# Other products to keep TensorE warm, shorter row-transfer times in the planner, and a new table of ranks

## The chip, the cores and the metric

The kernel runs on one core of a Trainium2 chip. The metric is the device time of one execution in microseconds (us). The kernel before was timed three times; the median is 1224.96 us (1224.6 to 1226.9). Engines are named as in the profile: PE is TensorE (PEld its weight loads), DVE is VectorE, ACT is ScalarE, POOL is GpSimd, SP is SyncE, which issues most DMAs.

## What is computed

A thresholded attention over 8 batches of 8 heads (576 tokens, head size 64), and then a feed-forward layer pair with a quick GELU over the 4608 tokens.

```python
scores = scale * np.matmul(q, k.transpose(0, 1, 3, 2))
thresh = np.max(scores, axis=-1, keepdims=True) - tau
scores = np.where(scores >= thresh, scores, -1000000000.0)
scores = scores - np.max(scores, axis=-1, keepdims=True)
attn = np.exp(scores)
attn = attn / (np.sum(attn, axis=-1, keepdims=True) + 1e-09)
x = np.matmul(attn, v)      # heads side by side: 4608 x 512
...
h = x @ w_in                # 512 x 2048
g = h * (1.0 / (1.0 + np.exp(-1.702 * h)))
return (g @ w_out).astype(np.float32)
```

All products run in FP32. The two weight matrices come as 64-bit floats.

## The kernel before

**Attention.** Two heads make a pair: there are 32 pairs, n = 0 to 31, four to a batch. A pair passes through these steps, each a function of that name:

- SP loads q, k and v (`load_qk`, `load_v`). The first four pairs are turned by TensorE (`turn_in`, L565 and L568) and copied out of PSUM by ScalarE (`turned`, L580) or VectorE (L578); later ones are transposed by VectorE (`prep`, L556).
- `scores_run` (L590) makes nine groups of scores, in the four 64 x 64 quadrants of the array at once. ScalarE copies each group to SBUF (`keep`, L607), VectorE takes maxima of blocks (`in_groups`, L613) and joins them (`over_tiles`, L622; `cross_max` on ScalarE, L632; `over_halves`, L639).
- The threshold has to be spread over the partitions. For pairs 1 and 3 to 6 that goes through DRAM: `turn_rows` (L646, L647) makes a row, `row_out` (L663) writes it, `row_in` (L672) reads it back to many partitions, and `add_row` (L678) adds it to two of the five score tiles by DMA. For pairs 0 to 7 these DMAs are issued by POOL. Pairs 0, 2 and 7 onwards use a VectorE transpose (`spread_max`, L651).
- `sub` (L687, VectorE) applies the threshold, `mask` (L694) and `exps` (L698) run on ScalarE, five tiles each. For pairs 0 to 3 TensorE makes the sums (`sums_by_pe`) and for all pairs the values (`values`), both through L709. `place_x` (L813) multiplies by the reciprocal and writes the input of the feed-forward part.

**Feed-forward.** 18 blocks of 256 tokens. The first two go together: `mm1_ahead` (L876) and `mm1_0` (L887), then the second layer (L856). They need pairs 0 to 3 placed and the first pieces of w_in. Later blocks use Strassen-like sums with seven products instead of eight (L955, L1097, L1248, L1357, L1397). From the seventh pair on, values of one pair and scores of the next run together on TensorE.

**Weights.** 16 pieces of w_in, then 16 of w_out, in 512 columns each, are loaded in that order (`load_w`, L510) and turned into FP32 by two ScalarE operations (`cv_power` L520, `cv_power2` L524) and two VectorE operations (`cv_whole` L538, `cv_end` L545).

**Warm products.** `run_up` (L1457) runs 32 product records on ones at the start. `stay_warm` (L1463) is a task of two products of 64 x 64 ones by 64 columns, both in the same quadrant of the array; each FP32 product leaves two records in the trace. 44 such tasks (`WARM`) stand behind pair 1's turned q and k, with the last rank of all. Their output is never read.

**The order.** The order on every engine is fixed when the kernel is built, by a planner in the kernel's own text, `run_in_order`. Every piece of work is a `task` with an engine, a cost in us, a rank, the tasks it comes after, and buffers that it takes and gives back (counted in `limits`). The planner plays time forward: whenever an engine is free it takes, among its tasks that are ready and whose buffers are free, the one with the lowest rank, and issues it. On the chip the engines then run these orders, each instruction waiting for what it really depends on.

The rank of an attention task is the pair's number plus a bias by function: `EARLY` for pairs 0 to 3, `SECOND` for 4 to 7, `LATER` above. `CV` biases the weight tasks, whose base goes linearly through `W_RANK` (first four pieces of w_in, the other twelve, w_out). `L_RANK` adds to the loads of q, k and v of pairs 0 to 7. Tasks of the feed-forward part have either the first rank of all (`FIRST`, -9) or 1000 (TensorE). Warm tasks have 1001.

DMA transfers are planned as tasks of two movers, DMS (queue of SP) and DMW (queue of POOL). For a row they are `row_out`'s issue, a transfer of 0.3 us with a lag, `row_in`'s issue, and a transfer of 1.1 us with a lag; `rq` holds for each pair the engine, a factor on the issue cost, the mover and the second lag, and `flow` an extra for the busy early stretch.

Of the kernel before, what the change touches and what calls it, by code (L numbers as in the profile page):

```python
# [21 lines left out]
P = 128  # L22
# [10 lines left out]
def kernel(  # L33
# [77 lines left out]
    ones = const.tile([P, D], FP32, name="ones")  # L111
# [7 lines left out]
    eye = const.tile([P, P], FP32, name="eye")  # L119
# [10 lines left out]
    for x in ("raw0", "raw1", "qkT0", "qkT1", "mb"):  # L130
# [3 lines left out]


    EARLY = {
        "add_row": 53.65,
        "cross_max": 41.92,
        "exps": 6.51,
        "in_groups": -32.22,  # L140
        "keep": -15.97,
        "load_qk": -22.11,
        "load_v": 171.75,
        "mask": 55.94,
        "one_row": -16.46,
        "over_halves": 4.98,
        "over_tiles": 6.84,
        "place_x": 20.81,
        "row_in": 57.26,
        "row_out": 46.57,  # L150
        "scores_run": -10.81,
        "spread_max": 80.7,
        "spread_sums": 100.15,
        "sub": 57.71,
        "sums_by_pe": -23.63,
        "turn_in": 17.28,
        "turn_rows": 22.22,
        "turned": 23.53,
        "values": 13.65,
    }  # L160
    SECOND = {
        "add_row": 56.43,
        "cross_max": 3.09,
        "cross_sums": 16.09,
        "exps": 52.27,
        "in_groups": 30.05,
        "keep": -234.91,
        "load_qk": -13.08,
        "load_v": -27.45,
        "mask": 33.62,  # L170
        "over_halves": 278.98,
        "over_tiles": -10.26,
        "place_x": -25.62,
        "prep": 26.79,
        "row_in": -17.52,
        "row_out": -29.19,
        "scores_run": -37.55,
        "spread_max": 47.26,
        "sub": 30.71,
        "sums_in": 55.32,  # L180
        "sums_out": 55.2,
        "turn_rows": -18.94,
        "turn_sums": 6.04,
        "values": -8.21,
    }
    LATER = {
        "add2": -48.46,
        "add3": -25.71,
        "copy2": 39.6,
        "copy3": -20.1,  # L190
        "cross_max": -23.15,
        "cross_sums": -92.97,
        "exps": 55.84,
        "in_groups": 20.69,
        "keep": -228.95,
        "load_qk": -18.31,
        "load_v": 17.97,
        "mask": 2.33,
        "over_halves": -43.91,
        "over_tiles": 0.85,  # L200
        "place_x": -1.66,
        "prep": 50.01,
        "s_level1": -3.36,
        "s_level2": -12.87,
        "scores_run": 9.86,
        "silu2": 26.22,
        "spread_max": 3.4,
        "sub": 4.36,
        "sums_in": 25.12,
        "sums_out": 39.44,  # L210
        "turn_sums": 63.21,
        "values": -6.31,
    }
# [34 lines left out]
    def transfer(by, time, a, kind=0, give=(), lag=1.7):  # L248
        return task(by, time, FIRST, moved, kind, after=[a], give=give, lag=lag)
# [1209 lines left out]
    def stay_warm(x):  # L1459

        d = psM.tile([P, BANK], FP32, name="up", tag="mo")
        for _ in range(2):
            nc.tensor.matmul(d[0:D, 0:D], lhsT=ones[0:KT], rhs=ones[0:KT], start=True, stop=True)  # L1463

    def tau_terms():

# [23 lines left out]
    ROWS_BY_POOL = range(8)  # L1490
# [38 lines left out]
    warmth = [task("PE", 4.4, -20.0, run_up, take=("psM",), give=("psM",))]  # L1529
# [760 lines left out]
    for n in range(NP):  # L2290
        gate = per_pair * (n - LEAD)
        assert gate < len(ffn) or gate <= 0
        after = [ffn[gate]] if gate >= 0 and ffn else []
        r = float(n)

        slow = 1.1 if n < 2 * NPAIR else 1.0
        rq = ("POOL", 1.4, "DMW", 2.2) if n in ROWS_BY_POOL else ("SP", 1.0, "DMS", 1.7)
        flow = 2.9 if n in (0, 1, 4) else 0.0
        by_sp = n not in ROWS_BY_POOL
        q0, q1 = (nc.scalar, nc.scalar) if n == 0 else (nc.sync, nc.sync)  # L2300

# [48 lines left out]
        if n >= JOINT:  # L2350

            a = None
            for t in range(NKT + 1):
# [12 lines left out]
                a = w  # L2366
                for j in js:
# [6 lines left out]
                    a = w  # L2374
# [141 lines left out]
```

## Time and profile before

| what | value |
|---|---|
| median of 3 runs | 1224.96 us (1224.6 to 1226.9) |
| the profiled execution | 1225.39 us |
| its span, first to last instruction | 1223.6 us |
| mean granted TensorE clock | 0.999 |
| records of L1463 (warm products) | 176, from 21.5 to 74.3 us, 13.1 us busy |
| records of L1457 (first products) | 32, 3.7 us busy |

How to read the profile: busy time of an engine is the time in which at least one of its instructions runs; a row of a stretch gives its borders and length, then busy time and number of instructions of PE, PEld, DVE, ACT and POOL, the granted TensorE clock, the busy share of the DMA engines and GB/s. A row of the timeline gives start, length, engine, line, operation, output and input, the number of instructions merged in it, and in brackets how long the engine stood idle before and what ended that. A row by line ends with busy time, mean ns of one, and idle time before it. Matmuls overlap, so their mean duration is longer than their share of the engine's time; rates are taken from rows with many records.

### The profile page before, as it was taken

How to read it: one execution, taken by the hardware profiler on the slowest of the kernel's cores; microseconds unless marked ns; L12 is line 12 of the kernel's file. 1: busy time of each engine (PE TensorE's matmuls, PEld its weight loads, DVE VectorE, ACT ScalarE, POOL GpSimd, SP SyncE). 2: the span in 40 equal slices, each digit the busy share in tenths (PEclk: the TensorE clock that was granted, in tenths of full speed). 3: DMA queues.
4: the chain of work that ended last, by engine and by line, in shares of the span. 5: the costliest groups of instructions: out<-in, count | busy, mean ns of one | idle time of the engine just before them, and what ended most of it. 6: DMA issues, size and time to landing. Idle time of an engine off the chain costs nothing.

```text
span 1223.6 us, 26039 instructions
## 1 busy us (share of the span) xinstructions
PE 1212.8 (99%) x10592; PEld 987.0 (81%) x10592; DVE 1059.3 (87%) x1649; ACT 803.1 (66%) x1203; POOL 71.0 (6%) x115
## 2 busy tenths in 40 slices
PE   9989999999999999999999999999999999999998
PEld 6857764597978888888777777778787797999998
DVE  6899966678898998898699977998799889999797
ACT  7999976676766756684786468756875676440340
POOL 0112231110000000000000000001100000000000
PEclk9999999999999999999999999999999999999999
DMA  7957779862323232224323252225322341444443
GB/s 203 252 108 199 196 146 190 209 100 58 101 49 110 49 116 56 75 77 126 101 66 103 71 128 76 65 65 128 91 50 67 101 125 50 129 130 141 141 134 103
DMA packets 202232, 137.12 MB, mean 112 GB/s; under 512 B 146880, under 2 KB 164416, under 8 KB 201984
## 3 DMA queue, kind: packets, MB, share of 16 engines
q1 hardware_dynamic: 189712, 110.21, 33.5%
q0 software_dynamic: 11712, 24.95, 10.1%
q8 instruction: 83, 1.36, 0.5%
q10 hardware_dynamic: 688, 0.30, 0.1%
q14 instruction: 37, 0.30, 0.1%
HBM read 103.28 MB, written 23.75 MB: 104 GB/s over the span
## 4 chain that ended last, share of the span: by engine, by line
PE 92%; ACT 4%; DMA 2%; DVE 1%; issue 0%; SPq 0%; POOL 0%; POOLq 0%
PE ops L1397 24%; PE pv L709 10%; PE ps L590 10%; PE hps L955 7%; PE hps L1097 7%; PE ps L955 5%; PE ps L1097 5%; PE ops L856 5%; PE hps L887 4%; PE ops L1357 4%; PE hps L1248 4%; PE ps L1357 3%; PE ps L1248 3%; ACT arena L694 1%; ACT arena L698 1%; ACT arena L607 1%
## 5 line engine op out<-in xcount | busy, mean ns | idle before, releaser
L613 DVE TRANSPOSE_TENSOR_REDUCE part<-arena 128x36 f32<-128x1152 f32 (+1 forms) x300 | 363.8, 1239 | 65.9 <-ACT arena L607 49.0
L607 ACT COPY arena<-ps 128x576 f32<-128x576 f32 x288 | 170.5, 644 | 96.8 <-PE ps L590 96.8
L694 ACT ACTIVATE arena<-arena 128x1152 f32<-128x1152 f32 (+1 forms) x160 | 165.1, 1060 | 67.7 <-DVE arena L687 67.5
L687 DVE TENSOR_TENSOR arena<-arena 128x1152 f32<-128x1152 f32 (+1 forms) x150 | 180.9, 1240 | 3.4 <-DMA arena<-row 2.8
L698 ACT ACTIVATE arena<-arena,shift 128x1152 f32<-128x1152 f32 (+1 forms) x160 | 180.5, 1154 | 1.5
L590 PE MATMUL ps<-arena 64*64 64x288 f32 x2304 | 171.4, 408 | 3.4 <-ACT arena L607 3.1
L1397 PE MATMUL ops<-w_out,arena 128*128 128x256 f32 x768 | 174.4, 381 | 0.0
L1397 PEld LDWEIGHTS ops<-w_out,arena 128*128 128x128 f32 x768 | 144.3, 190 | 24.9 <-issue 5.3
L709 PE MATMUL pv<-arena 64*64 64x288 f32 x2176 | 158.5, 405 | 0.0
L590 PEld LDWEIGHTS ps<-arena 64*64 64x64 f32 x2304 | 82.2, 132 | 64.1 <-ACT arena L607 25.3
L709 PEld LDWEIGHTS pv<-arena 64*64 64x64 f32 x2176 | 82.2, 133 | 52.2 <-issue 9.1
L1397 PE MATMUL ops<-arena 128*128 128x256 f32 x528 | 118.1, 379 | 0.0
L1397 PEld LDWEIGHTS ops<-arena 128*128 128x128 f32 x528 | 100.2, 190 | 14.0 <-issue 0.4
L1262 ACT COPY arena<-hps 128x512 f32<-128x512 f32 x44 | 25.7, 584 | 58.4 <-PE hps L1248 58.3
L632 ACT ACTIVATE other<-red,minus_gap 32x18 f32<-32x18 f32 x118 | 36.2, 307 | 39.0 <-DVE red L622 37.6
L856 PE MATMUL ops<-w_out,arena 128*128 128x512 f32 x128 | 55.9, 595 | 0.0
L1074 POOL DMA_DIRECT2D arena<-wrow x36 | 19.4, 540 | 596.8 <-DMA arena<-in_k_dram 299.6
L887 PE MATMUL hps<-xT,w_in 128*128 128x256 f32 x232 | 50.8, 380 | 0.0
L887 PEld LDWEIGHTS hps<-xT,w_in 128*128 128x128 f32 x232 | 43.9, 190 | 6.8 <-issue 0.4
L856 PEld LDWEIGHTS ops<-w_out,arena 128*128 128x128 f32 x128 | 24.1, 190 | 30.1 <-issue 29.5
L955 PEld LDWEIGHTS hps<-xT,w_in 128*128 128x128 f32 x384 | 44.2, 192 | 1.1 <-issue 0.9
L955 PE MATMUL hps<-xT,w_in 128*128 128x128 f32 x384 | 44.9, 275 | 0.0
(228 smaller groups left out, 1922.2 us busy)
## 6 DMA issues: line engine op xcount, KB each, us to landing
arena<-in_v_dram SPq DMA_DIRECT2D x128, 144.0 KB
arena<-exu SPq DMA_DIRECT2D x42, 256.0 KB
arena<-ext SPq DMA_DIRECT2D x39, 256.0 KB
arena<-wrow POOLq DMA_DIRECT2D x36, 256.0 KB, 3.0
arena<-in_k_dram SPq DMA_DIRECT2D x112, 72.0 KB
arena<-in_q_dram SPq DMA_DIRECT2D x112, 72.0 KB
out_dram<-osb SPq DMA_DIRECT2D x28, 256.0 KB
arena<-row_s SPq DMA_DIRECT2D x48, 144.0 KB
```

The source lines that it names most:

```text
L590: nc.tensor.matmul(ps[ts(c, KT), h, 0:SH], lhsT=mats[n, 1][ts(h, D), ts(j, KT)], rhs=mats[n, 0][ts(h, D), ts(c, SH)], start=True, stop=True,)
L607: nc.scalar.copy(out=sT[n, t][:, u], in_=pss.pop((n, j))[:, :, 0:SH])
L613: nc.vector.tensor_reduce(out=stats[n, op][:, t * 2 * QB : min(2 * t + 2, NK) * QB], in_=sT[n, t].rearrange("p u h (g d) -> p (u h g) d", ...
L687: engine.tensor_tensor(out=s, in0=s, in1=mbs[n].unsqueeze(1).to_broadcast(list(s.shape)), op=ALU.add if n in BY_DMA else ALU.subtract,)
L694: nc.scalar.activation(out=s, in_=s, func=AF.Prelu, alpha=STEEP)
L698: nc.scalar.activation(out=s, in_=s, func=AF.Exp, scale=SCALE, bias=shift)
L709: nc.tensor.matmul(o[c][ts(h, D), 0:SH], lhsT=left(j, h)[ts(c, KT)], rhs=sT[n, t][ts(c, KT), u, h, :], start=(j == 0), stop=(j == NK - 1),)
L856: nc.tensor.matmul(acc[i], lhsT=g0[:, j, ts(i, P)], rhs=w_out[:, j, :], start=(j == 0), stop=(j == NFC - 1),)
L887: nc.tensor.matmul(hidden[j][:, ts(i, BLK)], lhsT=w_in[:, c, ts(j, P)], rhs=xTs[i][:, c, :], start=(c == 0), stop=(c == NDC - 1), skip_gro ...
L955: nc.tensor.matmul(o[:, ts(j, HT)], lhsT=left[:, c, ts(4 * y + j, P)], rhs=right[:, c, :], start=(x in (P1, P2, P5) and j + c == 0), stop= ...
L1097: nc.tensor.matmul(o[:, ts(j, BLK)], lhsT=left[:, c, ts(j, P)], rhs=right[:, c, :], start=(x in (P1, P2, P5) and j + c == 0), stop=(j + c ...
L1397: nc.tensor.matmul(banks[blk][k][:, ts(o, HM)], lhsT=left[:, j, :], rhs=right[:, j, :], start=(j == 0), stop=(j == HF - 1),)
```

## The change

The warm products use two diagonal quadrants in turn, 128 columns of the identity wide; there are 40 tasks instead of 44, planned at 0.24 us instead of 0.26.

```diff
     def stay_warm(x):
         d = psM.tile([P, BANK], FP32, name="up", tag="mo")
-        for _ in range(2):
-            nc.tensor.matmul(d[0:D, 0:D], lhsT=ones[0:KT], rhs=ones[0:KT], start=True, stop=True)
+        for r in range(2):
+            nc.tensor.matmul(
+                d[ts(r, KT), 0:P], lhsT=ones[ts(r, KT)], rhs=eye[ts(r, KT)], start=True, stop=True
+            )
...
-    WARM = 44
+    WARM = 40
...
-                    "PE", 0.26, LAST + 1.0, stay_warm, x, after=warmth[:1] + [pq, pk],
+                    "PE", 0.24, LAST + 1.0, stay_warm, x, after=warmth[:1] + [pq, pk],
```

The planner's figures for the row transfers of pairs whose rows go by POOL become shorter; `flow` no longer holds for pair 4.

```diff
-        rq = ("POOL", 1.4, "DMW", 2.2) if n in ROWS_BY_POOL else ("SP", 1.0, "DMS", 1.7)
-        flow = 2.9 if n in (0, 1, 4) else 0.0
+        rq = ("POOL", 1.4, "DMW", 1.0) if n in ROWS_BY_POOL else ("SP", 1.0, "DMS", 1.7)
+        flow = 2.9 if n in (0, 1) else 0.0
...
-            a = transfer(rq[2], 0.3 + 0.4 * by_sp, task(rq[0], 0.65 * rq[1], r, row_out, n, after=[a]), lag=1.7 - 0.4 * by_sp + flow)
+            a = transfer(rq[2], 0.3 + 0.4 * by_sp, task(rq[0], 0.65 * rq[1], r, row_out, n, after=[a]), lag=1.3 + flow)
```

All tables of ranks are replaced. The entries that the prediction speaks of, and some beside them:

```diff
     EARLY = {
-        "in_groups": -32.22,
-        "mask": 55.94,
-        "scores_run": -10.81,
-        "spread_max": 80.7,
-        "sub": 57.71,
-        "sums_by_pe": -23.63,
-        "turn_in": 17.28,
-        "values": 13.65,
+        "in_groups": 34.28,
+        "mask": 36.88,
+        "scores_run": -51.59,
+        "spread_max": 71.02,
+        "sub": -16.81,
+        "sums_by_pe": 32.0,
+        "turn_in": 64.69,
+        "values": 84.4,
...
     SECOND = {
-        "exps": 52.27,
-        "keep": -234.91,
-        "mask": 33.62,
-        "prep": 26.79,
-        "scores_run": -37.55,
+        "exps": 388.41,
+        "keep": -169.42,
+        "mask": 33.53,
+        "prep": 138.87,
+        "scores_run": 61.18,
...
     LATER = {
-        "over_halves": -43.91,
-        "prep": 50.01,
-        "sums_in": 25.12,
+        "over_halves": -352.38,
+        "prep": 370.61,
+        "sums_in": -380.05,
...
     CV = {
-        "cv_end": 32.35,
-        "cv_power": 11.31,
-        "cv_power2": 54.89,
-        "cv_whole": 26.47,
-        "load_w": 23.87,
+        "cv_end": -85.19,
+        "cv_power": -24.57,
+        "cv_power2": 42.72,
+        "cv_whole": 54.77,
+        "load_w": 75.9,
...
-    W_RANK = (76.72, 196.12, 138.01, 508.95, -9.25, -19.99)
+    W_RANK = (0.79, 73.66, 64.74, 576.72, -32.54, 123.84)
...
-    L_RANK = (3.45, -109.6, -17.9, 36.14, 35.53, 42.62, 27.86, 146.49, 9.14, 81.46, 255.02, -17.35, -3.34, -15.75, -2.02, -2.69, 30.05, -3.25, -48.27, 6.8, -9.58, 10.21, 37.91, -22.41)
+    L_RANK = (-12.89, -5.54, 219.74, 60.65, 2.71, 44.19, 8.15, 170.96, -56.11, 65.12, 219.59, 54.4, 32.1, -27.46, 84.01, -13.31, 4.97, 33.77, 16.65, 59.15, -8.32, 117.45, -4.08, 3.78)
```

More of the change, by code (lines that the diff above doesn't have):

```diff
@@ L136 @@
     EARLY = {
-        "add_row": 53.65,
-        "cross_max": 41.92,
-        "exps": 6.51,
-        "in_groups": -32.22,
-        "keep": -15.97,
-        "load_qk": -22.11,
-        "load_v": 171.75,
-        "mask": 55.94,
[L145 to L150, printed above, removed]
-        "scores_run": -10.81,
-        "spread_max": 80.7,
-        "spread_sums": 100.15,
-        "sub": 57.71,
@@ L155 @@
-        "sums_by_pe": -23.63,
-        "turn_in": 17.28,
-        "turn_rows": 22.22,
-        "turned": 23.53,
-        "values": 13.65,
+        "add_row": 16.2,
+        "cross_max": 0.85,
+        "exps": 5.8,
+        "in_groups": 34.28,
+        "keep": -13.29,
+        "load_qk": -44.57,
+        "load_v": -92.15,
+        "mask": 36.88,
+        "one_row": -17.5,
+        "over_halves": -19.66,
+        "over_tiles": 26.01,
+        "place_x": 48.08,
+        "row_in": -17.7,
+        "row_out": -73.39,
@@ L160 @@
+        "scores_run": -51.59,
+        "spread_max": 71.02,
+        "spread_sums": 71.54,
+        "sub": -16.81,
+        "sums_by_pe": 32.0,
+        "turn_in": 64.69,
+        "turn_rows": 25.43,
+        "turned": 40.57,
+        "values": 84.4,
     }
     SECOND = {
-        "add_row": 56.43,
-        "cross_max": 3.09,
-        "cross_sums": 16.09,
-        "exps": 52.27,
-        "in_groups": 30.05,
-        "keep": -234.91,
-        "load_qk": -13.08,
-        "load_v": -27.45,
-        "mask": 33.62,
@@ L171 @@
-        "over_halves": 278.98,
-        "over_tiles": -10.26,
-        "place_x": -25.62,
-        "prep": 26.79,
-        "row_in": -17.52,
-        "row_out": -29.19,
-        "scores_run": -37.55,
[L178 to L184, printed above, removed]
+        "add_row": 60.51,
+        "cross_max": 65.99,
+        "cross_sums": 93.45,
+        "exps": 388.41,
@@ new lines @@
+        "in_groups": 15.92,
+        "keep": -169.42,
+        "load_qk": -2.78,
+        "load_v": 45.15,
+        "mask": 33.53,
+        "over_halves": 106.16,
+        "over_tiles": 173.93,
+        "place_x": 0.35,
+        "prep": 138.87,
+        "row_in": -36.73,
+        "row_out": -28.75,
+        "scores_run": 61.18,
+        "spread_max": -62.9,
+        "sub": -0.08,
+        "sums_in": 33.43,
+        "sums_out": 16.98,
+        "turn_rows": 30.64,
+        "turn_sums": 58.3,
+        "values": 36.63,
@@ L185 @@
     }
     LATER = {
[L187 to L198, printed above, removed]
-        "over_halves": -43.91,
-        "over_tiles": 0.85,
-        "place_x": -1.66,
-        "prep": 50.01,
-        "s_level1": -3.36,
-        "s_level2": -12.87,
@@ L205 @@
[L205 to L208, printed above, removed]
-        "sums_in": 25.12,
-        "sums_out": 39.44,
-        "turn_sums": 63.21,
-        "values": -6.31,
+        "add2": -78.59,
+        "add3": -21.16,
+        "copy2": -2.96,
+        "copy3": 10.29,
+        "cross_max": 29.07,
+        "cross_sums": 9.97,
+        "exps": 51.04,
+        "in_groups": 16.36,
+        "keep": -125.24,
+        "load_qk": -53.63,
+        "load_v": 23.85,
@@ L213 @@
+        "mask": 76.05,
+        "over_halves": -352.38,
+        "over_tiles": -124.45,
+        "place_x": -29.68,
+        "prep": 370.61,
+        "s_level1": -19.31,
+        "s_level2": -19.31,
+        "scores_run": 21.7,
+        "silu2": 3.69,
+        "spread_max": 55.41,
+        "sub": -9.37,
+        "sums_in": -380.05,
+        "sums_out": -6.37,
+        "turn_sums": 51.16,
+        "values": 114.47,
     }
     CV = {
-        "cv_end": 32.35,
-        "cv_power": 11.31,
-        "cv_power2": 54.89,
```

## The prediction

> **What bounds the kernel now.** I read the page first: busy shares, then the slices.
>
> ```profile
> span 1223.6 us, 26039 instructions
> ...
> PE 1212.8 (99%) x10592; PEld 987.0 (81%) x10592; DVE 1059.3 (87%) x1649; ACT 803.1 (66%) x1203; POOL 71.0 (6%) x115
> ...
> PE   9989999999999999999999999999999999999998
> ...
> ACT  7999976676766756684786468756875676440340
> ```
>
> TensorE is the bound over the whole run, but ScalarE is full in slices 1 to 4 only, and just there TensorE is not quite full. So the next view is busy time by stretches of 20 us and more (columns: length, then PE, PEld, DVE, ACT, POOL with counts, the granted clock, DMA).
>
> ```profile
> 20.00:40.00 20.00, 17.93 (x296) 14.83 (x296) 17.78 (x22) 19.73 (x31) 6.09 (x8) 0.94 1.00 256
> 40.00:60.00 20.00, 20.00 (x321) 18.22 (x318) 18.13 (x34) 19.02 (x26) 0.00 (x0) 0.97 0.97 246
> 60.00:80.00 20.00, 17.61 (x248) 10.27 (x248) 18.66 (x24) 19.87 (x29) 5.87 (x8) 1.00 0.57 111
> 80.00:100.00 20.00, 18.79 (x268) 10.37 (x264) 17.81 (x39) 19.77 (x26) 4.37 (x8) 1.00 0.56 119
> 100.00:120.00 20.00, 19.86 (x114) 16.45 (x111) 19.83 (x29) 19.92 (x31) 2.61 (x4) 1.00 0.85 219
> ...
> 500.00:600.00 100.00, 100.00 (x878) 82.50 (x876) 85.01 (x127) 59.69 (x92) 4.38 (x8) 1.00 0.40 108
> ```
>
> From 20 to 100 us ScalarE is 95 to 99% busy, while TensorE has holes and the filler products besides. From about 105 us to the tail TensorE has no hole, and nothing in the diff takes work from it there. Whatever this change is worth is therefore decided by the moment when the dense feed-forward stream begins. The chain that ended last shows that moment (start, length, what):
>
> ```profile
> 100.39 0.67 ACT w_in L520
> 101.06 0.54 ACT arena L607
> 101.64 0.71 PE ps L590 x8
> 102.36 1.06 PE hps L887 x4
> ```
>
> ScalarE's copy of scores (L607) releases the last scores of pair 5, and the first layer (L887) follows at 102.36. Before that the chain runs on ScalarE. What ScalarE did between 14 and 102 us, by line:
>
> ```profile
> L607 ACT COPY arena<-ps 128x576 f32<-128x576 f32 x45 | 26.5, 655 | 0.0
> L698 ACT ACTIVATE arena<-arena,shift 128x1152 f32<-128x1152 f32 (+1 forms) x20 | 23.3, 1166 | 0.5
> L694 ACT ACTIVATE arena<-arena 128x1152 f32<-128x1152 f32 (+1 forms) x20 | 21.3, 1066 | 0.8 <-DVE arena L687 0.8
> L524 ACT ACTIVATE w_in<-w_in,rebias 128x512 int32<-128x512 f32 x10 | 7.1, 720 | 0.0
> L520 ACT ACTIVATE w_in<-w_out,rebias 128x512 f32<-128x512 int16 x8 | 6.3, 784 | 0.0
> ...
> L520 ACT ACTIVATE w_in<-arena,rebias 128x512 f32<-128x512 int16 x4 | 3.1, 771 | 0.0
> ```
>
> The first layer needs pairs 0 to 3 and four pieces of w_in (eight of the 22 conversions). Not needed are 18 of the 45 copies (pairs 4 and 5) and 14 conversions, whose work is displaced in time, not saved.
>
> **The warm products.** These are TensorE's rows around them:
>
> ```profile
> 20.45 1.26 PE L568 MATMUL ps<-eye,arena 64*64 64x64 f32 x36
> ...
> 30.11 1.26 PE L590 MATMUL ps<-arena 64*64 64x288 f32 x16
> ...
> 32.05 4.39 PE L1463 MATMUL up<-ones 64*64 64x64 f32 x68
> 37.51 2.27 PE L568 MATMUL ps<-eye,arena 64*64 64x64 f32 x32 [1.06 <-DMA arena<-in_k_dram]
> ...
> 44.70 4.71 PE L709 MATMUL pv<-arena 64*64 64x288 f32 x72
> ...
> 50.03 0.83 PE L590 MATMUL ps<-arena 64*64 64x288 f32 x8
> ```
>
> One task leaves four records; 68 records in 4.39 us are 0.258 us a task. The new product has no row. L568 runs in two diagonal quadrants already: 36 records in 1.26 us are 0.035 us each, so four of 64 columns take 0.14 us, and of 128 columns at most twice that, 0.28 us. From below, L709 moves 72 records of 288 columns through four quadrants in 4.71 us; two quadrants and 128 columns give 4 x 0.0654 x 2 x 128/288 = 0.116 us. I take 0.24, near the upper end, since small products cost more per column. Forty tasks are 9.6 us against 44 x 0.258 = 11.4 us now. They fill time in which TensorE waits for ScalarE or a transfer, so I count 0; without that cover it would be -1.8 us, or at the ends -6.8 and -0.2 us.
>
> **The clock.** The half-microsecond stretches around the gap at 36.4 us:
>
> ```profile
> 37.50:38.00 0.50, 0.39 (x4) 0.26 (x6) 0.50 (x2) 0.50 (x1) 0.50 (x2) 0.74 1.00 401
> 38.00:38.50 0.50, 0.50 (x11) 0.50 (x12) 0.50 (x2) 0.50 (x1) 0.50 (x2) 0.50 1.08 409
> ...
> 41.00:41.50 0.50, 0.50 (x13) 0.50 (x9) 0.50 (x2) 0.50 (x1) 0.00 (x0) 0.85 1.02 262
> 41.50:42.00 0.50, 0.50 (x14) 0.50 (x10) 0.50 (x2) 0.47 (x2) 0.00 (x0) 1.00 1.06 298
> ```
>
> The granted clock is 0.5 for some 3.3 us, right after 4.39 us of one-quadrant products and 1.06 us of nothing. The transposes of pair 3's k, 32 records in 2.27 us, take 1.0 us longer than 36 did at 20.45. VectorE and ScalarE behind them:
>
> ```profile
> 40.12 0.76 DVE L578 COPY arena<-ps 128x576 f32<-128x576 f32 x1 [1.62 <-PE ps L568]
> ...
> 44.35 1.35 DVE L687 TENSOR_TENSOR arena<-arena 128x1152 f32<-128x1152 f32 x1
> ...
> 53.65 0.45 DVE L622 TENSOR_REDUCE red<-part 128x18 f32<-128x162 f32 x1
> ```
>
> ```profile
> 42.22 0.77 ACT L520 ACTIVATE w_in<-arena,rebias 128x512 f32<-128x512 int16 x1
> ...
> 44.27 0.71 ACT L524 ACTIVATE w_in<-w_in,rebias 128x512 int32<-128x512 f32 x1
> 45.74 1.16 ACT L694 ACTIVATE arena<-arena 128x1152 f32<-128x1152 f32 x1 [0.76 <-DVE arena L687]
> ```
>
> VectorE stood 1.62 us in front of L578, with pair 1's subtraction (L687, 44.35) queued behind, and ScalarE stood 0.76 us. Busier products (two quadrants, twice the columns) can keep the clock up, and the new ranks put fewer weight pieces ahead of pair 3's k. Bounds 0 and -0.76; I take -0.5 us.
>
> The Trainium skill, "TensorE: Matmul & The Clock Gate", Part 1, says that the clock is halved after an idle window of about 3.4 us. The length of the slow stretch agrees (3.3 us); the cause does not, as only 1.06 us were empty. If the window counted the products as busy, the quadrants would change nothing, this term would be 0 and the sum 0.5 us higher.
>
> **The order.** Nothing is computed differently; ranks decide what an engine takes first. Three shifts can be read off the table of ranks. On TensorE scores of early pairs drop to -51.6, below their sums (32) and pair 3's turn-in (64.7). A pair's nine score groups are 72 records of L590. Today eight of pair 2's are done with the row at 30.11 and the ninth runs at 50.03, behind pair 0's sums and values, so pair 2's maximum is known at 53.65 only. Moved ahead, it gives ScalarE masks to do between 42.22 and 44.98, where it converted weights for want of them. That filler is 2.76 us; VectorE must still reduce pair 2 first, so I leave one conversion (0.71) and take -2.0 us (bounds 0 and -2.76). On VectorE the subtraction drops to -16.8, below the maxima (34): pairs end one after another; no price beside the above. The transposes of pairs 4 to 7 (prep) go from 26.8 to 138.9, so pair 5's scores probably come after the start of the first layer. That relieves ScalarE of nine copies, and costs TensorE the scores later:
>
> ```profile
> 9.35 4.98 ACT L607 COPY arena<-ps 128x576 f32<-128x576 f32 x9 [0.91 <-PE ps L590]
> ```
>
> Nine copies are 5.0 us; 72 records at the rate of the 72 above are 4.7 us. Net -0.3 us (0 to -5.0, if TensorE finds a hole for them). SP's loads change places (v of pair 1 right behind v of pair 0, before w_in 3), which I price at 0 within the bounds of pair 3's k; ranks after 105 us at 0, as TensorE has no hole to close there.
>
> **The row transfers.** The planner's figures for the row of a pair on POOL's queue become shorter. What the trace has (start, length, issue; and time from issue to landing):
>
> ```profile
> 26.54 1.05 POOL L663 DMA_DIRECT2D row<-flat  x2 [24.20 <-DVE flat L647]
> 34.09 0.54 POOL L672 DMA_DIRECT2D arena<-row  x1 [6.49 <-DMA row<-flat]
> 34.91 0.53 POOL L672 DMA_DIRECT2D arena<-row  x1 [0.28 <-DMA row<-flat]
> ...
> DMA to landing us min/median/max: 7.2/7.2/7.3
> ```
>
> Pair 1's row took from 26.54 to 34.91 + 7.2 = 42.1, so 15.6 us. The new constants give 0.91 + 0.3 + 1.3 + 2.9 and 1.54 + 1.1 + 1.0 + 2.9, 11.9 us; the old ones 13.5. I count 0, with +3.7 us as the upper bound (first rival).
>
> **Sum.** -0.5 - 2.0 - 0.3 = -2.8 us against the profiled execution's 1225.39 us (span 1223.6 and 1.8 around it) is 1222.6; the median of the runs is 0.43 lower, so 1222.2 us.
>
> **Rivals.**
> *Slower: VectorE at pair 1's row.* If the planner puts pair 1's subtraction where its row is due, VectorE stands up to 15.6 - 11.9 = 3.7 us, with the reductions of pairs 2 and 3 queued behind, and ScalarE runs out. 1224.96 + 3.7 = 1228.7 us. For it: the old, longer figure was already too short by 2.1 us. Against: the row landed at 42.1 and the subtraction began at 44.35, so VectorE had other work then. It decides as soon as fewer than 3.7 us of other VectorE work are ordered ahead of that subtraction.
>
> *Slower: the quadrants do not overlap.* Then a record of 128 columns takes what the full-array product of that width takes.
>
> ```profile
> L955 PE MATMUL hps<-xT,w_in 128*128 128x128 f32 x384 | 44.9, 275 | 0.0
> ```
>
> 44.9/384 is 0.117 us, four are 0.47, forty tasks 18.7 us, 7.3 more than now; unhidden 1232. L568 speaks against it.
>
> *No difference.* ScalarE's stretch is as long in any order, since its work for pairs 0 to 3 is the same and fillers only change places: 1225 us. For it: in the four stretches from 20 to 100 us ScalarE stands only 1.6 us in all.
>
> *Much faster.* Of the 14 conversions not needed half are put off, 7 x 0.75 (16.5 us for 22) = 5.2 us, beside the sum: 1217.0 us. Against: the later pieces already rank behind the early pairs today.
>
> **How the numbers follow.** Forecast 0.40 (own range 1220 to 1224.8), row rival 0.24, quadrants 0.06, no difference 0.14, much faster 0.16. A measurement of this kernel can tell about 0.2%, 2.45 us, from no change. The forecast lies just beyond that: 0.25 faster, 0.12 same, 0.03 slower. Faster is 0.25 + 0.16 = 0.41; same 0.12 + 0.13 = 0.25; slower 0.03 + 0.24 + 0.06 + 0.01 = 0.34. The range runs from 1216 (just below the much faster case) to 1230 (above the row rival), leaving out the unhidden quadrants and the open end of the order's bounds.
>
> **What would show it.** Right: the granted clock stays at 1.0 from 30 to 45 us; four records of L1463 in about 0.24 us; the ninth score group of pair 2 before pair 0's sums; fewer than four conversions between exponentials of pair 0 and masks of the next; L887 from about 99.5 us. Wrong: VectorE idle 2 to 4 us before L687 at 38 to 45 us with the row as releaser (row rival); L887 later than 102.4; or TensorE holes after 105 us, which I priced at nothing.

## The result, and the profile after

The changed kernel takes 1230.01 us (median of 6 runs, 1228.34 to 1230.72) against 1224.78 of the kernel before beside it (6 runs, 1223.73 to 1226.9): a ratio of 1.0038, interval 1.0025 to 1.0051. It is slower by some 5 us, and the profiled executions say the same: 1230.66 us and a span of 1228.9, against 1225.39 and 1223.6, so 5.3 us are to be found in the trace.

The page of the kernel after, TensorE's 40 slices:

```profile
PE   8999899999999999999999999999999999999999
```

The fifth slice (123 to 154 us) is no longer full. The stretches of 20 us, with the columns of the prediction's table:

```profile
20.00:40.00 20.00, 17.88 (x312) 11.97 (x308) 19.74 (x25) 19.77 (x32) 5.89 (x8) 1.00 0.97 298
...
120.00:140.00 20.00, 16.91 (x178) 11.75 (x177) 15.97 (x29) 16.10 (x29) 8.13 (x12) 0.97 0.86 187
140.00:160.00 20.00, 20.00 (x89) 17.46 (x88) 19.15 (x32) 18.43 (x26) 3.47 (x7) 0.94 0.69 201
```

Up to 120 us nothing is lost. From 120 to 140 TensorE, VectorE and ScalarE all stand for 3 to 4 us, where TensorE had no hole before. TensorE's timeline after:

```profile
104.89 16.57 PE L887 MATMUL hps<-xT,w_in 128*128 128x256 f32 x76
...
130.29 5.45 PE L887 MATMUL hps<-xT,w_in 128*128 128x256 f32 x24
138.83 29.58 PE L887 MATMUL hps<-xT,w_in 128*128 128x256 f32 x128 [3.09 <-DVE arena L893]
168.25 1.88 PE L856 MATMUL ops<-w_out,arena 128*128 128x512 f32 x4
```

The first layer starts its dense run at 104.89, 0.95 us earlier than before (105.84), and then stands 3.09 us for VectorE's GELU step (L893). VectorE and POOL at that place:

```profile
132.98 0.95 DVE L813 TENSOR_TENSOR xT<-pv,arena 128x192 f32<-128x192 f32 x4 [0.86 <-DMA arena<-row_s]
136.82 1.36 DVE L687 TENSOR_TENSOR arena<-arena 128x1152 f32<-128x1152 f32 x1 [2.89 <-DMA arena<-row]
138.10 0.68 DVE L893 SCALAR_TENSOR_TENSOR arena<-xT,hps 128x512 f32<-128x512 f32 x1
```

```profile
124.61 1.01 POOL L663 DMA_DIRECT2D row<-flat  x2
...
128.94 0.53 POOL L672 DMA_DIRECT2D arena<-row  x1 [0.79 <-DMA row<-flat]
131.68 0.54 POOL L672 DMA_DIRECT2D arena<-row  x1 [2.21 <-DMA row<-flat]
```

Time from issue to landing, of the write's two DMAs (L663) and of the read's (L672):

```profile
DMA to landing us min/median/max: 4.0/4.9/5.7
...
DMA to landing us min/median/max: 4.9/5.0/5.1
```

Pair 5's row is on its way from 124.61 to 136.8, 12.2 us. The planner's new figures for this pair add up to 0.91 + 0.3 + 1.3 and 1.54 + 1.1 + 1.0, 6.2 us. VectorE comes to the first of pair 5's subtractions (L687) at 133.93, 9.3 us after the write's issue, stands there for 2.89 us, and the GELU step that TensorE waits for stands behind it. In the same trace the writes of pairs 3, 4 and 6 landed in 1.6 to 1.7 us, as the new figure says. What is different for pair 5 is seen on SP's queue:

```profile
124.32 1.05 SPq L510 DMA_DIRECT2D arena<-in_moe_w_out_dram  x2
...
129.87 2.42 SPq L468 DMA_DIRECT2D arena<-in_v_dram  x4
```

Two pieces of w_out (1 MB) are issued just ahead of the row's write, and v of pair 6 beside its read. Write and read of the row (first and last start of their DMAs) and their landing times in the kernel before:

```profile
L663 POOL DMA_DIRECT2D row<-flat x2: 546/549/552, 117.8 to 118.4; - x2
...
DMA to landing us min/median/max: 3.2/3.2/3.2
...
L672 POOL DMA_DIRECT2D arena<-row x2: 527/530/533, 121.3 to 121.9; - x2
...
DMA to landing us min/median/max: 4.3/4.4/4.5
```

From 117.8 to 121.9 + 4.5 = 126.4 the row took 8.6 us there, and it landed 1.4 us ahead of the first of pair 5's three subtractions in VectorE's timeline before:

```profile
127.78 1.35 DVE L687 TENSOR_TENSOR arena<-arena 128x1152 f32<-128x1152 f32 x1
```

That is 9.9 us after the write's issue, against 9.3 now. So the shorter figures and the new order together took only 0.6 us from the room that the row has; the row itself became 3.6 us longer. The pieces of w_out alone are not the whole difference, since the same two were issued 0.84 us ahead of the write in the kernel before as well (SP's queue):

```profile
117.00 2.02 SPq L510 DMA_DIRECT2D arena<-in_moe_w_out_dram  x2
```

There SP had issued nothing for 5.7 us; after the change k of pair 7 goes out just ahead of the pieces (120.99 us) and q behind them (125.42), and the row of pair 4's sums is written and read on POOL's queue beside pair 5's (123.42 and 126.93).

The hole costs more than its length. The single microseconds behind it:

```profile
138.00:139.00 1.00, 0.17 (x1) 0.17 (x2) 1.00 (x3) 0.79 (x1) 0.00 (x0) 0.93 1.10 198
139.00:140.00 1.00, 1.00 (x3) 0.82 (x4) 1.00 (x2) 0.86 (x2) 0.00 (x0) 0.50 0.75 136
...
142.00:143.00 1.00, 1.00 (x6) 0.90 (x5) 1.00 (x2) 0.91 (x2) 0.00 (x0) 0.86 0.83 278
```

For 3.4 us the granted clock is 0.5, some 1.7 us of work. So 3.09 + 1.7 - 0.95 = 3.8 us, and that is how much later the second layer's first product (L856) starts, with the same work done: 168.25 against 164.46. The other 1.5 us of the 5.3 go behind that.

The Trainium skill, "TensorE: Matmul & The Clock Gate", Part 1, gives for the clock's step down an idle window of about 3.4 us that is free-running. The length of the slow stretch agrees (3.4 us); the gap in front of it (3.09) was a little shorter than the window.

### The profile page after: what moved, and what is told of

Its sections match the earlier page's. It is cut to its first block, busy times and chain, and to the rows that moved or that the text cites. A ratio compares the mean times of both kernels' runs of the same rounds, so it can differ in the third digit from the quotient of the medians.

```text
span 1228.9 us, 25942 instructions
## 1 busy us (share of the span) xinstructions
PE 1213.6 (99%) x10576; PEld 977.0 (80%) x10576; DVE 1059.3 (86%) x1649; ACT 817.3 (67%) x1209; POOL 71.3 (6%) x115
## 4 chain that ended last, share of the span: by engine, by line
PE 78%; ACT 8%; DMA 2%; DVE 2%; issue 1%; POOL 0%; DVEq 0%; ACTq 0%; SPq 0%; POOLq 0%
PE ops L1397 23%; PE pv L709 9%; PE ps L590 8%; PE hps L955 6%; PE ps L955 5%; PE hps L1248 4%; PE ops L1357 4%; PE hps L1097 4%; PE ps L1248 3%; PE ps L1357 3%; PE ps L1097 3%; PE ops L856 3%; PE hps L887 2%; ACT arena L698 2%; ACT arena L694 2%; ACT arena L1148 1%
## 5 line engine op out<-in xcount | busy, mean ns | idle before, releaser
L694 ACT ACTIVATE arena<-arena 128x1152 f32<-128x1152 f32 (+1 forms) x160 | 169.1, 1062 | 59.8 <-DVE arena L687 56.6
L698 ACT ACTIVATE arena<-arena,shift 128x1152 f32<-128x1152 f32 (+1 forms) x160 | 185.6, 1162 | 3.5
L687 DVE TENSOR_TENSOR arena<-arena 128x1152 f32<-128x1152 f32 (+1 forms) x150 | 180.5, 1245 | 4.3 <-DMA arena<-row 3.5
L887 PE MATMUL hps<-xT,w_in 128*128 128x256 f32 x232 | 53.0, 390 | 3.1 <-DVE arena L893 3.1
L856 PE MATMUL ops<-w_out,arena 128*128 128x512 f32 x128 | 55.9, 595 | 0.0
L887 PEld LDWEIGHTS hps<-xT,w_in 128*128 128x128 f32 x232 | 45.0, 196 | 11.0 <-DVE arena L893 3.5
L856 PEld LDWEIGHTS ops<-w_out,arena 128*128 128x128 f32 x128 | 24.1, 190 | 30.0 <-issue 29.2
```

The source lines that it names most:

```text
L687: engine.tensor_tensor(out=s, in0=s, in1=mbs[n].unsqueeze(1).to_broadcast(list(s.shape)), op=ALU.add if n in BY_DMA else ALU.subtract,)
L694: nc.scalar.activation(out=s, in_=s, func=AF.Prelu, alpha=STEEP)
L698: nc.scalar.activation(out=s, in_=s, func=AF.Exp, scale=SCALE, bias=shift)
L856: nc.tensor.matmul(acc[i], lhsT=g0[:, j, ts(i, P)], rhs=w_out[:, j, :], start=(j == 0), stop=(j == NFC - 1),)
L887: nc.tensor.matmul(hidden[j][:, ts(i, BLK)], lhsT=w_in[:, c, ts(j, P)], rhs=xTs[i][:, c, :], start=(c == 0), stop=(c == NDC - 1), skip_gro ...
```

## The experiments

"Frozen" means that the order which the planner made for the changed kernel is kept, and only the named tasks change place; `behind(a, b)` puts b right behind a. Ratios are against the kernel before on the same chip.

**Which part of the change costs?** The old products in the changed kernel, and the new products in the kernel before:

```diff
-        for r in range(2):
-            nc.tensor.matmul(
-                d[ts(r, KT), 0:P], lhsT=ones[ts(r, KT)], rhs=eye[ts(r, KT)], start=True, stop=True
-            )
+        for _ in range(2):
+            nc.tensor.matmul(d[0:D, 0:D], lhsT=ones[0:KT], rhs=ones[0:KT], start=True, stop=True)
```

> The changed kernel with the old warm products (two of 64 columns in one quadrant), still 40 tasks in the same places. If the two quadrants cost or gain nothing (they fill holes): 1230 us, within 1 us. If they keep the clock up between 20 and 45 us: it falls to half somewhere there, as it did in the kernel before at 37.5 us, and the time is 0 to 2 us longer. If the wider products delay useful work: 1228 to 1229 us.

1229.74 us, 1.0035 (1.0023 to 1.0048): the same loss with the old products. The wait on the GELU step was 2.5 us in this execution, and the clock stayed up behind it (its waits of TensorE, then the stretch behind):

```profile
PE hps L887 <- DVE arena L893: 2.5, 1, 2.5
```

```profile
140.00:160.00 20.00, 20.00 (x93) 17.38 (x92) 19.83 (x33) 19.66 (x28) 4.03 (x7) 1.00 0.71 204
```

So the half clock is not part of every execution; the hole is. From 20 to 50 us the clock stayed at 1.00 with the old products too, against the second expectation: in the new order it does not need the new ones.

> The kernel before with the new warm products alone, 44 tasks in the old order, old ranks and old planner times. If the slow clock at 37.5 us came from products that count as idle: the clock stays at 1.0 although TensorE still stands up to 1 us at pair 3's k, and the time is 0 to 1.5 us shorter than before, 1223.3 to 1224.8 us. If it came from the gap: the clock falls again, 1224.8 us. If the products run longer than the old ones and push work: slower than 1225.5 us.

1224.45 us, 0.9998 (0.9988 to 1.0009): no gain. TensorE's timeline of this kernel, and a stretch of 2 us behind the gap:

```profile
31.75 4.41 PE L1463 MATMUL up<-eye,ones 64*64 64x128 f32 x68
38.85 0.29 PE L568 MATMUL ps<-eye,arena 64*64 64x64 f32 x2 [2.69 <-DMA arena<-in_k_dram]
```

```profile
40.00:42.00 2.00, 2.00 (x36) 2.00 (x38) 0.48 (x1) 1.97 (x4) 0.00 (x0) 0.50 1.03 243
```

68 records of two-quadrant products run right up to the gap, and the clock is halved behind it all the same. But the gap was longer in this execution than in the kernel before (2.69 us against 1.06), so what the products would do in front of a gap of 1.06 us is not shown.

The changed kernel's order without any warm product:

```diff
+        issued = [i for i in issued if tasks[i][3] is not stay_warm]
```

> The changed kernel in its own order without any of the 40 warm products. If they only fill holes and the clock would stay up without them: 1230 us, within 1 us, minus nothing for the two at the end. If the clock needs them: it is at half for one or more stretches of 3.3 us between 20 and 100 us; that stretch is set by ScalarE, so the time is 0 to 3 us longer, 1230 to 1233 us.

1230.39 us, 1.0038 (1.0025 to 1.0052). The clock does fall here, and the median is that of the changed kernel within its interval; ScalarE is full in that stretch:

```profile
20.00:40.00 20.00, 14.84 (x220) 8.18 (x216) 19.78 (x23) 19.70 (x34) 5.88 (x8) 0.83 0.97 302
```

The planner's new row figures in the kernel before, and the old ones in the changed kernel:

```diff
-        rq = ("POOL", 1.4, "DMW", 2.2) if n in ROWS_BY_POOL else ("SP", 1.0, "DMS", 1.7)
-        flow = 2.9 if n in (0, 1, 4) else 0.0
+        rq = ("POOL", 1.4, "DMW", 1.0) if n in ROWS_BY_POOL else ("SP", 1.0, "DMS", 1.7)
+        flow = 2.9 if n in (0, 1) else 0.0
```

> The kernel before with the planner's new row-transfer times alone (old ranks, old products). Theory: shorter times put subtractions earlier than rows land, so VectorE stands at a row (L687 waiting for the row by DMA) somewhere before 170 us and the time is 1 to 6 us longer, 1226 to 1231 us. Rival (the new ranks are to blame, not the times): within 1 us of 1224.8 us.

1261.99 us, 1.0298 (1.0284 to 1.0312). A miss of both: 36 us slower, but not at the rows (L687 waits 2.4 us for them).

```profile
PE ops L856 <- DVE w_out L545: 14.8, 3, 12.0
```

TensorE's largest wait (us in total, times, longest) is for a converted piece of w_out. The other way round:

> The changed kernel with the planner's old row-transfer times (new ranks, new products). If ranks are good only together with the times that they were searched with: far slower, 1240 to 1280 us, with waits in many places, as the old ranks with the new times were (1262). If longer times simply move pair 5's subtraction to where its row lands: no wait at L687, 1225 to 1227 us.

1258.27 us in a single execution. Both mixtures are some 30 us slower than either kernel: a table of ranks fits only the figures it was found with, presumably since one task placed otherwise shifts all that follow. "One part alone" does not price a part in such a kernel, and the next experiments freeze the order.

**Is it the row, and would another order hide it?** Pair 5's first two subtractions moved behind the GELU step that TensorE waits for:

```diff
+        behind(find("gelu_0", 7), find("sub", 5, 0), find("mask", 5, 0), find("sub", 5, 1), find("mask", 5, 1))
```

> The changed kernel in its own order, with one edit: the first two subtractions and masks of pair 5 are put behind the activation of the eighth group of the first layer (gelu_0, j = 7), so that VectorE no longer stands at pair 5's row in front of the work that TensorE needs. Theory (the row of pair 5 is late, 3.1 us of TensorE idle and 3.3 us at half clock behind it): the hole at 135.7 us goes, the clock stays at 1.0, and the time is 3.09 + 1.65 = 4.7 us shorter than the changed kernel's 1230.0, about 1225.3 us. Rival (the new order is worse all along, the hole only where it shows first): VectorE or ScalarE run short a little later, and less than 2 us come back: 1228 us or more. Rival (the warm products cost it): no change, 1230 us.

1229.64 us, 1.0034 (1.0022 to 1.0047): the hole moves and the time stays. VectorE's and TensorE's timelines:

```profile
134.50 0.95 DVE L827 TENSOR_TENSOR xT<-pv,arena 128x192 f32<-128x192 f32 x4 [2.17 <-DMA arena<-row_s]
```

```profile
145.22 22.67 PE L901 MATMUL hps<-xT,w_in 128*128 128x256 f32 x96 [1.96 <-DVE arena L907]
```

Now `place_x` stands 2.17 us for the row of pair 4's sums (row_s), and TensorE stands 1.96 us one block later. `place_x` has its old place in the order, where it waited 0.86 us in the changed kernel, so part of this hole is a row_s that came later in this execution. VectorE and ScalarE are full from 105 us on, so it is likely that a time in which VectorE stands cannot be made up by another order on VectorE, and that the rows themselves have to come earlier.

The transfers beside the rows taken out. This kernel leaves out the loads of v of pair 6 and of pieces 20 and 21 (w_out's fifth and sixth); their tiles keep what was in them.

```diff
+                ) if n != 6 else None
...
+        if i not in (20, 21):
+            nc.sync.dma_start(
```

> The changed kernel with three loads left out, so that the tiles keep earlier data: the v of pair 6 and pieces 4 and 5 of w_out, 1.6 MB that are issued between 124 and 132 us, around pair 5's row. Theory (pair 5's row lands late behind these transfers, and the late row is what costs): row out and in together take about 6 to 8 us instead of 12.2, VectorE stands less than 1 us at L687, no hole at 135.7 us and no half clock, time 1225 to 1226.5 us. Rival (row is late from its own queue or from the transfers of sums): the row stays late and the time stays within 1 us of 1230. Rival (VectorE and ScalarE are simply full here): the row lands in time, a hole comes some 5 to 10 us later, 1228 us or more.

1225.76 us, 1.0004 (0.9995 to 1.0013). The landing times of write and read, then VectorE's and TensorE's timelines:

```profile
DMA to landing us min/median/max: 2.3/2.6/2.9
...
DMA to landing us min/median/max: 3.5/3.7/3.9
```

```profile
133.43 1.33 DVE L688 TENSOR_TENSOR arena<-arena 128x1152 f32<-128x1152 f32 x1
...
163.75 1.88 PE L857 MATMUL ops<-w_out,arena 128*128 128x512 f32 x4
```

No wait for the row is left, no hole, and the second layer starts at 163.75, 4.5 us earlier than in the changed kernel and 0.7 earlier than before. Of the loss, this is the larger part.

Nothing left out, but the two pieces loaded behind v of pair 6, and their conversions later:

```diff
+        behind(find("load_v", 6), find("load_w", 20), find("load_w", 21))
+        behind(find("mask", 5, 4), find("cv_power", 20), find("cv_power", 21))
+        behind(find("prep", 7, 1), find("cv_whole", 20))
```

> The changed kernel with nothing left out: pieces 4 and 5 of w_out are issued behind the v of pair 6 instead of ahead of pair 7's q, and their conversions follow later. Theory: the first half of pair 5's row (the write to DRAM) lands in about 2 to 3 us instead of 4.3 and 5.7, the second half still meets v; VectorE's wait at L687 falls by 2 to 3 us, and the time by 1 to 4 us, 1226 to 1229 us. Rival: the transfers only change places, 1230 us.

1227.49 us, 1.0021 (1.0012 to 1.0030). Write and read of the row land in 2.5 and 3.2 us, and the subtraction waits for nothing: of the three loads it is the pieces of w_out, in their place between the other loads, that held the row up. They are missed elsewhere instead (waits of TensorE, then its timeline):

```profile
PE hps L903 <- DVE arena L909: 0.9, 2, 0.7
```

```profile
165.79 1.88 PE L872 MATMUL ops<-w_out,arena 128*128 128x512 f32 x4
```

2.5 us are won back of 3.8.

**Where are the other 1.5 us?** Behind 168 us the changed kernel's TensorE stands 0.53 us at 250 us and 0.93 us at 885, 1.46 us together, both times for score copies; before, it stood 0.03 us in the whole of 800 to 900. After:

```profile
800.00:900.00 100.00, 99.01 (x762) 77.75 (x761) 83.77 (x113) 70.94 (x103) 6.45 (x12) 1.00 0.37 97
```

ScalarE goes to and fro there between silu (L1148) and exponentials (L698), and each turn takes a table load:

```profile
869.92 1.28 ACT L1148 ACT_TABLE_LOAD   x1
874.39 1.28 ACT L698 ACT_TABLE_LOAD   x1
876.96 1.28 ACT L1148 ACT_TABLE_LOAD   x1
882.63 1.28 ACT L698 ACT_TABLE_LOAD   x1
```

Four kernels tried two edits at once, the exponentials of pair 26's tile 3 behind the eight silu, and the `t_minus` of block 2 behind score copies of pair 9:

```diff
+        behind(next(i for i in issued[issued.index(e) :] if tasks[i][3].__name__ == "silu4" and tasks[i][4] == (1, 0, 1)), e)
+        behind(find("keep", 9, 1), find("t_minus", 2, 0))
+        behind(find("keep", 9, 3), find("t_minus", 2, 1))
```

They compute two things otherwise: the sums over that tile are taken ahead of its exponentials, and half of one of block 2's sums of w_out lacks the addition of `t_plus`.

> The changed kernel's order with two edits on ScalarE alone: the exponentials of pair 26, tile 3, behind the eight silu of block 4 (no table load between them, where the changed kernel has three loads of 1.28 us from 869.92 to 876.96), and the two t_minus of block 2 (L997) behind the first four score copies of pair 9. Theory (the 1.5 us lost behind 168 us are waits of TensorE for late score copies, 0.93 at 885 and 0.53 at 250, the first from table loads): both waits gone, two table loads of 1.28 us fewer, TensorE idle under 0.3 us in 800 to 900 us (0.99 in the changed kernel), 1228.8 us. Rival (the 1.5 us are spread over denser or sparser products, the waits only show them): waits move elsewhere, 1230.2 us.

> The same two edits, and the loads of w_out pieces 20 and 21 behind v of pair 6 with their conversions later, as in x6_w_out_later (1227.49 us). Theory: both savings add up, 1226.0 us, still over the kernel before's 1224.8. Rival: the second saving is lost later, 1227.5 us.

> The same two edits, and the loads of w_out pieces 20 and 21 only two loads later: behind q of pair 7 and ahead of v of pair 6, conversions where they were. Theory (the row is late for what was issued shortly before each of its two transfers): the write of the row lands in 2.5 us or less instead of 4.0 to 5.7, its read still in 4.5 to 5; the subtraction waits for the row about 1 us or less, TensorE's hole is under 1.5 us and the clock stays at 1.0; 1226.0 us. Rival (any megabyte of loads in this stretch holds the row up alike): hole 3 us as in the changed kernel, 1228.8 us.

> The same two edits in x7_three_loads_out (leaves out the loads of v of pair 6 and of pieces 20 and 21 of w_out; 1225.76 us). Theory (row at 137 us and two late stretches of score copies are the whole loss): 1224.4 us, the kernel before's time or a little under it, so that all other ranks and the products are worth within 0.5 us. Rival (something else also costs): 1225.7 us.

1238.67, 1235.81, 1238.36 and 1234.64 us (1.0103, 1.0082, 1.0103 and 1.0071): all 8 to 9 us slower than the kernels they start from, which neither theory nor rival had. The second `t_minus` had been put behind `t_plus` of the same sum, a DMA by POOL that writes the same tile. In the first of the four:

```profile
250.15 1.57 POOL L1018 DMA_DIRECT2D arena<-w_out  x1 [21.18 <-PE ps L607]
...
259.04 1.06 ACT L1014 ACTIVATE arena<-arena 128x1024 f32<-128x1024 f32 x1 [8.12 <-DMA arena<-w_out]
...
260.67 2.20 PE L607 MATMUL ps<-arena 64*64 64x288 f32 x16 [7.82 <-ACT arena L624]
```

It waits 8.12 us for that transfer, the score copies stand behind it, and TensorE stands 7.82 us: the accident of pair 5's row again, on ScalarE's queue. The times of these four therefore answer nothing about the 1.5 us. Two readings hold in spite of it. From 800 to 900 us TensorE stands 0.34 us instead of 0.99, about what the first edit should bring (forecast: under 0.3). And in the third kernel, with the pieces of w_out loaded behind q of pair 7, the row's write lands in 2.4 us as forecast, but its read in 7.2 to 7.3: the place of the loads decides which of the two transfers is slow. The hole at 139 us is 2.5 us there, with `place_x` waiting 2.00 us for row_s, against the forecast of under 1.5.

The first edit alone, with the sum behind it:

```diff
+        behind(next(i for i in issued[issued.index(e) :] if tasks[i][3].__name__ == "silu4" and tasks[i][4] == (1, 0, 1)), e, s)
```

> The changed kernel's order with one edit alone: the exponentials of pair 26, tile 3, and the sum over them on VectorE behind the eight silu of block 4. Theory (the hole of 0.93 us at 885 comes from the table loads that alternate there): no hole over 0.2 us from 870 to 895, two table loads fewer, 800 to 900 us with TensorE idle 0.34 us as in x9_two_orders against 0.99, and 1229.6 us. Rival (the hole is a matter of the copies' order): it stays, 1230.2 us.

1230.83 us, 1.0047 (1.0030 to 1.0065). There are two table loads fewer, 0.34 us of the hole near 885 are left (forecast: under 0.2), and from 800 to 900 us TensorE stands 0.34 us in all, as expected. But in this execution the hole at pair 5's row was the largest seen (TensorE's timeline):

```profile
140.82 29.52 PE L903 MATMUL hps<-xT,w_in 128*128 128x256 f32 x128 [4.55 <-DVE arena L909]
```

The 0.65 us are seen in the trace. In the time they cannot be seen, against a row whose hole is 2.31 us (first of the four kernels above) to 4.55 us from one execution to the next in the same order.

> The same edit in x6_w_out_later (1227.49 us). Theory: 1226.9 us, still over the kernel before's 1224.8 to 1226.2; rival: 1227.5 us.

1227.52 us, 1.0017 (1.0008 to 1.0027), which decides nothing between 1226.9 and 1227.5.

> The same edit in x7_three_loads_out (1225.76 us; leaves out the loads of v of pair 6 and of pieces 20 and 21 of w_out). Theory (row at 137 us and late score copies are the whole loss): 1225.1 us, within 0.1% of the kernel before on the same chip. Rival: 1225.8 us or more.

1225.34 us, 0.9999 (0.9990 to 1.0009), and a span of 1223.6 us, that of the kernel before. TensorE's timeline and the stretches:

```profile
163.74 1.88 PE L873 MATMUL ops<-w_out,arena 128*128 128x512 f32 x4
```

```profile
170.00:300.00 130.00, 129.59 (x995) 81.80 (x992) 102.72 (x145) 100.24 (x143) 17.86 (x20) 1.00 0.73 151
800.00:900.00 100.00, 99.66 (x766) 78.53 (x765) 84.08 (x116) 69.07 (x102) 6.45 (x12) 1.00 0.37 93
```

With the rows undisturbed and one of the late holes mended, the changed kernel is level with the kernel before. It is 0.7 us ahead at the second layer, and gives that back in small waits later (0.41 us from 170 to 300, 0.34 from 800 to 900, where the kernel before has 0.00 and 0.03). Of the 1.5 us, 0.65 go with two table loads fewer in the trace; the rest is spread over waits of under 0.6 us that were not tried one by one, and stays open. No version that computes everything was found to beat the kernel before.

## Why the prediction was wrong

**The step that failed** is "ranks after 105 us at 0, as TensorE has no hole to close there", together with the rows' "I count 0". "No hole to close" was true, and the wrong question: new ranks can open one. They moved pair 5's row from 117.8 to 124.6 us, and pair 4's values and pair 6's scores some 16.5 us ahead (121.4 us instead of 137.9), into a stretch where VectorE and ScalarE are full and SP loads k, q, v and w_out. There the row took 12.2 us instead of 8.6. In the terms of the sum: where it has -2.8 us, the early terms made -0.95, and the term at 0 made 3.09 us of hole, 1.7 of half clock and 1.5 behind 168 us.

The first rival had the kind of wait, VectorE standing at a subtraction with its other work queued behind. That its price, 3.7 us, is near what the first 168 us lost (3.8) is luck: it was worked out for pair 1 at 38 to 45 us, and there VectorE stood for 0.64 us after the change:

```profile
41.54 3.90 DVE L687 TENSOR_TENSOR arena<-arena 128x1152 f32<-128x1152 f32 x3 [0.64 <-DMA arena<-row]
```

Nor was its reason, figures shorter than the row takes, what made the hole at pair 5: they and the new order took 0.6 us of the row's room, and the row itself became 3.6 us longer. The trace of before could have raised the question, with pair 5's row at 8.6 us against the old figure of 7.75 and the new one of 6.2. It also has a wait of the same size, at pair 6's row:

```profile
173.36 2.63 DVE L687 TENSOR_TENSOR arena<-arena 128x1152 f32<-128x1152 f32 x2 [2.79 <-DMA arena<-row]
```

TensorE has no hole there (20.00 us of 20 from 160 to 180), so a late row costs only where something that TensorE needs soon stands behind its waiter.

The new figure of the write, 1.6 us, is that of rows that run undisturbed, and how long a row takes depends on the loads that the planner itself puts beside it. A longer figure alone would probably not have helped much: the old one, 7.75, is short of 12.2 as well. Without the two pieces beside it the row does land in time (2.5 and 3.2 us); which of the other transfers makes these pieces cost more than they did in the kernel before was not tried.

**The products** were rightly counted at 0 (0.9998 in the kernel before). Their cost, 0.24 us a task, was slightly under what the trace has; four records make a task:

```profile
21.80 2.62 PE L1463 MATMUL up<-eye,ones 64*64 64x128 f32 x40
```

That is 0.262 us, or 0.0655 for a record of 128 columns, against 0.117 in the rival in which the quadrants do not overlap.

**The clock** (-0.5 us): it did stay at 1.0 from 20 to 45 us, as forecast, but not for the first of the two reasons given, busier products: with the old ones in the changed kernel the clock stays at 1.00 too, and only without any does it fall (0.83 from 20 to 40 us). The second reason fits: pair 3's k comes earlier, and TensorE does not stand for it. Whether busier products would have helped in front of the gap of before is not shown. (By the prediction's own rows the slow stretch lasts 0.26 + 3.0 + 0.15 = 3.4 us, not 3.3.) The step's price cannot be told apart from the next one: all early terms together, forecast at -2.8, made -0.95 at the start of the dense stream, and in other executions of this order that start lies between 105.09 and 105.83 us, so that less or nothing is left of it. The sign "L887 from about 99.5 us" is met by two records at 99.86, and means little, since the dense run begins at 104.89.

**The order** (-2.0 us) half happened and brought little. The ninth score group of pair 2 was to run ahead of pair 0's sums. Eight groups do, and the sums begin at 35.30; the ninth is still the eight records at 47 us:

```profile
46.97 0.40 PE L590 MATMUL ps<-arena 64*64 64x288 f32 x1
...
47.21 0.71 PE L590 MATMUL ps<-arena 64*64 64x288 f32 x7
```

A rank of -51.6 ranks only what is ready with its buffers free. The kernel's text says which buffer it is: the ninth group fills the fifth score tile, pairs 0 and 2 share a single one (`"s_t0": 1` in `limits`), and pair 0 gives it back only with the last of its values, which end at 45.6. Even so ScalarE does no conversion between pair 0's exponentials and pair 1's masks, which follow each other at 43.1. The conversions have only changed places: from 14 to 101 us it does 24 of them, against 22 before (14 to 102). Pair 5's scores (-0.3 us) were not put off either: its last three groups run at 100.90, between the first products of L887. ScalarE is busy 19.8 us of every 20 (before: 19.0 to 19.9), so the rival "no difference" was nearest for this stretch: its work stays the same whatever the order.

## What to carry to other kernels

A planner's figure for a transfer is only as good as the traffic it was measured in: compare the room between its issue and its use with every instance of that transfer in the trace, the busiest first, and judge a late one by who stands behind its waiter on the same in-order engine. Where the engines around the bound one were full, moving the waiter moved the hole; moving the traffic closed it. And ranks found by search belong to the costs they were found with: exchange one without the other and this kernel loses some 30 us, so freeze the order before pricing a part.

## What the runs showed of the hardware that was not expected

The write of a row of a few KB on POOL's queue takes two to three and a half times as long when a megabyte is issued on SP's queue just ahead of it: it lands in 3.2 us (before) and in 4.0 to 5.7 us (after) instead of 1.6. Its read, to many partitions, lands in up to 7.3 us instead of 3.1. Both times also differ between executions of one order, which makes the hole behind it 2.31 to 4.55 us.

The granted clock was halved behind gaps of 1.06 us (before), 1.96 us (pair 5's subtractions moved), 2.69 us (new products in the kernel before) and 3.09 us (after), and not behind one of 2.5 us (old products in the changed kernel) nor one of 1.29 us in the changed kernel itself. The length of a gap alone does not tell. In the clock records of the traces every change of the clock lies a whole number of steps of 3.41 us behind its first rise, whenever the gap began: the clock fell at 37.74 us in the kernel before and at 138.86 after, for one step each, and without warm products twice, for two steps each. So what counts seems to be how busy TensorE was in a whole step. In the last one ahead of the fall it was busy for 0.32 us (after), 0.73 (new products in the kernel before) and 1.46 (subtractions moved); where the clock stayed up, the emptiest step around the hole had 1.54 us (third of the four kernels) and 1.67 (old products in the changed kernel). The kernel before does not fit: 2.35 us busy, and the clock fell. But 2.11 of these were one-quadrant products, so it may be that these count for less than the others; no run tells.
